# TensorE in place of VectorE for the turns of q and x in blocks 1 and 2, and block 3's q loaded in block 1's down stage

## The chip, the cores and the metric

The kernel runs on one core of one Trainium2 chip. The metric is the device time of one execution in microseconds (us), lower is better. All data is float32.

## The reference

Linear attention with a normalization, followed by a gated feed-forward block. The attention's output is laid out as one row of 512 values per token.

```python
# q, k, v: (8 batches, 8 heads, 576, 64)
kv  = einsum('bhsd,bhse->bhde', k, v)
o   = einsum('bhsd,bhde->bhse', q, kv)
o   = o / sqrt(mean(o * o, axis=-1) + 1e-6) * g_norm
x   = o.transpose(0, 2, 1, 3).reshape(4608, 512)
g   = x @ w_gate                      # (512, 1536)
out = (g / (1 + exp(-g)) * (x @ w_val)) @ w_out   # w_out (1536, 512)
```

## The kernel before

**Blocks and stages.** The 4608 tokens are worked off in nine blocks (0 to 8) of 512. Block n has an *up* stage (the gate and value products into `h`, 1536 wide) and a *down* stage (`h` times `w_out`, stored to `out`). While block n's down stage runs, the attention of block n + 1 (`nxt`, an object of class `Att`) is computed between its products, so that x of the next block is ready when its up stage begins.

**Products.** Block 0's up stage is a plain product (`plain_up`, L1018). From block 1 on, products are split after Strassen and Winograd into seven products of half size, called P1 to P7, each with sums of operands. Class `Up` does this once for block 1; class `Inner` does it twice, one inside the other, from block 2 on (`DEEP = 2`); class `Down` does it for the down stage. All these matmuls are issued at L551 (`Quad.multiply`) or L714 (`Inner.multiply`). The order of the products in the down stage is the list in `Ffn.down`; after a product p, `fill[p]` runs a piece of the next block's attention.

**The weights' stream.** The inner products need sums of weight pieces ("leaves"). They are made once, in block 1, by `leaf_steps` on VectorE (the steps show as L111 and L112) and written to DRAM by SP's queue (L823). From block 2 on `Stream.pump` loads them from there into `t` tiles (L795), as fast as these nine tiles come free; `Stream.enable`, called behind P7 of the down stage before, begins this. The leaves of the last two of six weight tiles (j = 4 and 5) are in `latest` and made in block 1's down stage, behind P5 in the x pool's `xi` tile and behind P7 in a tile of its own. Block 2's own sums of x, `xi`, are written into that same `xi` tile afterwards.

**Loads of q and k, v.** They pass through a pool `ld` of four tiles. All of these loads, the leaves and the stores go through SP's queue, in one order.

**The next block's attention.** `TURNED` and `quarters` choose between two ways of turning q and x (tokens on partitions) into q and x with features on partitions:

- With `quarters`, q is loaded in pieces of 32 by 32 (`load_quarters`, L282: two DMAs for most pieces, 32 for a block's q), turned within these squares by one VectorE step for each half (L329), and needs no TensorE. Without it, q is loaded in rows (L298), turned by 16 TensorE transposes (L335) and copied out of PSUM by VectorE (L339) or ScalarE (L337).
- From block `TURNED` on, `steps` runs `whole` behind P1: the product of q and kv in one piece (L355), its squares (L366) and sums (L367), one inverse root (`root`, 11 small VectorE steps, L373 to L385), the scaling (L113), and two VectorE turns (`blocks_x`, L412). Behind P5 `place_x` moves the 32-wide squares to their places by 16 DMAs on SP and ACT (L426), and behind P2 `gain_x` (L433) and `sums` follow. Before block `TURNED`, the block is done in two halves: `half(0)` behind P1, `middle` behind P6 (`turn_x(0)` and `half(1)`) and `last` behind P2 (`turn_x(1)` and `sums`). `turn_x` turns by 8 TensorE transposes (L402) and two ScalarE copies with the gain (L403).

In the kernel before, `TURNED` is 1 and `quarters` holds for every block but 0, so block 0 alone uses TensorE for turns.

**Order.** The program is written in the order above; a scheduler then sets the order of instructions of each engine by its own costs. `tc.issue_after(...)` lets the code in its body be ordered only behind a given instruction. `t2` prepares the weights that block 1's products use, in block 0's down stage; `turn_t(p)` makes three tiles of weight differences on GpSimd for the down stage's products P5, P7 and P4; P4's waits for the next block's first half. PSUM pools: `a` 1 tile, `b` 3, `c` 2, `m` 2.

Of the kernel before, what the change touches and what calls it, by code (L numbers as in the profile page):

```python
# [8 lines left out]
F32 = mybir.dt.float32  # L9
# [5 lines left out]
P = 128  # L15
# [3 lines left out]
def kernel(  # L19
# [41 lines left out]
    nc = tc.nc  # L61
# [22 lines left out]
    ld_pool = pool("ld", 4)  # L84
# [27 lines left out]
    sub = lambda e, o, a, b: e.tensor_tensor(out=o, in0=a, in1=b, op=OP.subtract)  # L112
    mul = lambda e, o, a, b: e.tensor_tensor(out=o, in0=a, in1=b, op=OP.mult)  # L113

    def ring():

        return r_pool.tile([P, 4, BLK], F32, name="r")
# [75 lines left out]
    class Att:  # L193


        def __init__(self, n):
            self.n = n

            self.cut, half = divmod(n, 2)
            self.split = half * D  # L200
            self.ps, self.z = {}, None
            self.q, self.k, self.v, self.room = [], {}, {}, None
            self.halves = []
            self.quarters = n > 0

        def parts(self, t):

# [58 lines left out]
                    )  # L266
                    views[j] = t.rearrange("p h (t d) -> p h t d", t=KT)

        def load_quarters(self, i, pairs=(0, 1)):


            if pairs[0] == 0:
                self.q.append(ld_pool.tile([P, LD], F32, name="ld")[:, 0 : 2 * BLK])
            to = self.q[i].rearrange("p (j g d) -> p j g d", j=2, d=P // 4)
            cut = 2 * self.n
            spans = [(self.n - 1, S - D * self.n, 0, cut), (self.n, 0, cut, BLK // 32)]
            for j in pairs:
                for r in range(4):
                    h, d = divmod(r, 2)
                    for b, s0, g0, g1 in spans:  # L280
                        if g1 > g0:
                            nc.sync.dma_start(  # L282
                                out=to[32 * r : 32 * (r + 1), j, g0:g1],
                                in_=q[b, 4 * i + 2 * j + h, s0 : s0 + 32 * (g1 - g0), 32 * d : 32 * (d + 1)].rearrange(
                                    "(g p) d -> p g d", p=32
                                ),
                            )

        def load_q(self, i):
            if self.quarters:  # L290
# [127 lines left out]
        def place_x(self):  # L418
            src = self.turned.rearrange("p i (x c) -> p (i x) c", c=P)
            self.x = x_pool.tile([P, 7, 2, HB], F32, name="x")  # L420
            dst = self.x[:, 0:4].rearrange("p o k (t c) -> p (o k t) c", c=P)
            rows = [slice(32 * r, 32 * (r + 1)) for r in range(4)]
            for a in range(4):
                for b in range(4):
                    queue = nc.scalar if b % 2 else nc.sync
                    placed = queue.dma_start(out=dst[rows[b], :, rows[a]], in_=src[rows[a], :, rows[b]])  # L426
                    if b % 2 == 0:
                        self.placed = placed

        def gain_x(self):  # L430
            for i in range(2):
# [93 lines left out]

    DEEP = 2

    TURNED = 1

    class Quad:  # L530

# [41 lines left out]
    class Up(Quad):  # L573
# [51 lines left out]
        def multiply(self, p):  # L625
            super().multiply(p)
            ffn = self.ffn
            if ffn.n != DEEP - 1:
                return

            if p == 5:
                self.leaf_room = ring().rearrange("p f (s c) -> p (f s) c", c=P)
            if p in (5, 7, 4):
                at = 3 * (5, 7, 4).index(p)
                ffn.making.extend(leaf_steps(self.j, [(self.w[p].unsqueeze(1), (p,))], self.leaf_room[:, at:]))
            if p == 3:
                if ffn.leaf_room is None:
                    ffn.leaf_room = x_pool.tile([P, 3, 7, P], F32, name="xi").rearrange("p a b c -> p (a b) c")
                halves = lambda t: t[self.j].rearrange("p (o i) c -> p o i c", o=2)
                steps = lambda room: leaf_steps(self.j, [(halves(wg), (1, 2)), (halves(wv), (6, 3))], room)  # L640
                if self.j < NP - 2:
                    ffn.later.extend(steps(ffn.leaf_room))
                else:
                    ffn.latest.append(steps)

# [195 lines left out]
    class Down(Quad):  # L841
# [51 lines left out]
        def after2(self):  # L893
            add(nc.vector, self.o1[:, :, 0:HD], self.ps["a"], self.s)
            if self.final:
                self.ffn.store(self.o1[:, :, 0:HD], 0, slice(0, HD))

            pairs = self.ffn.h.rearrange("p (j e) t -> p e j t", e=2)
            self.s4 = sub(nc.vector, pairs[:, 1, :, 0:HB], pairs[:, 1, :, 0:HB], pairs[:, 0, :, HB:BLK])

        def after7(self):
            o = ring()
# [25 lines left out]
    class Ffn:  # L928
# [52 lines left out]
        def down(self, nxt):  # L981

            down = self.down_
            fill = nxt.steps() if nxt else {}
            for p in (1, 6, 5, 7, 2, 4, 3) if 5 in fill else (1, 5, 6, 7, 2, 4, 3):
                if p == 1:
                    down.turn_t(7, self.ended)
                if p == 6:
                    down.turn_t(4, nxt.halves[0] if nxt and nxt.n >= TURNED else None)

                with tc.issue_after(nxt.multiplied.ins) if self.n == 0 and p in (5, 6) else ExitStack():
                    down.multiply(p)
                self.make(12)
                if p in fill:
                    fill[p]()
                if p in (5, 7) and self.n == DEEP - 1:

                    with tc.issue_after(nxt.scaled.ins), tc.issue_after(nxt.placed.ins):
                        room = self.leaf_room if p == 5 else ring().rearrange("p f (s c) -> p (f s) c", c=P)
                        for step in self.latest.pop(0)(room):  # L1000
                            step()
                if p == 1:

                    with tc.issue_after(nxt.q_turned.ins) if self.n == 0 else ExitStack():
                        down.turn_s3()
# [60 lines left out]
    for n in range(NB):  # L1066
        ffn = Ffn(n, blocks[n])
        nxt = blocks[n + 1] if n + 1 < NB else None
        if n == 0:

            with tc.issue_after(squared.ins), tc.issue_after(scaled.ins):
                weights(2)
            ffn.plain_up(0, (0,))
            copied = blocks[0].copied
            blocks[0].turn_x(1)
            for f in range(NF):
                with tc.issue_after(blocks[0].copied.ins if f else copied.ins):
# [12 lines left out]
            ffn.plain_end()  # L1090
            for g in range(2):
                nxt.kv(g)
        else:

            def third():
                nxt.kv(0)
                nxt.load_kv(1)

            def two_thirds():
                nxt.kv(1)  # L1100
                if nxt.n == 2:
# [12 lines left out]
        if DEEP <= n < NB - 2:  # L1114
            for i in range(2):
                blocks[n + 2].load_q(i)
        ffn.down(nxt)
        if n == 0:
            blocks[2].load_kv(0)

            with tc.issue_after(nxt.halves[0].ins):
                for j in range(NP // 2):
                    t2(wv[j][:, 0:2], wv[j][:, 2:4], wg[j][:, 0:2])
            with tc.issue_after(ffn.down_.s4.ins):
                for j in range(NP // 2, NP):
                    t2(wv[j][:, 0:2], wv[j][:, 2:4], wg[j][:, 0:2])


# [29 lines left out]
```

## Time and profile before

| what | value |
|---|---|
| time, median of 3 runs | 1025.14 us (1025.01 to 1025.32) |
| the profiled execution's own time | 1025.01 us |
| its span | 1023.2 us |
| TensorE (PE) busy | 1006.5 us, 98% |
| VectorE (DVE) busy | 701.0 us, 69% |
| ScalarE (ACT) / GpSimd (POOL) busy | 228.0 / 368.9 us |
| granted TensorE clock | 1.00 |

The page gives the busy time of each engine, the share of each in the chain of work that ended last, and groups of instructions by source line. The busy sum of PE is of the records' lengths laid over each other; matmuls are pipelined, so what one costs is read from the distance between starts. In an answer of the timeline a row is: start, length, engine, line, operation, out <- in, shape, count, and in brackets how long the engine was idle before it and who released it. In the waits a row is: total us, how often, the longest. SPq and ACTq are the queues in which an engine issues DMAs. A line L111, L112 or L113 is that of a helper (add, subtract, multiply) and tells the operation only.

### The profile page before, as it was taken

Reading aid. Unit: us, or ns where it says so; the run is one execution under the profiler, and the core shown is the slowest. Engines: PE = TensorE matmul, PEld = TensorE weight load, DVE = VectorE, ACT = ScalarE, POOL = GpSimd, SP = SyncE. Lnnn points to the kernel's source line nnn. Section 1 sums busy time; section 2 is a strip of 40 time slices with the busy share of each in tenths; the row PEclk is TensorE's granted clock in tenths of the full one; section 3 lists DMA queues with packets and bytes.
Section 4 is the critical chain, followed back from the end, with each engine's and each line's share of the span. In section 5 each row is a group of like instructions: output and inputs, shape, how many; then the busy total and the mean of one; then the engine's idle time right before and its main releaser. Section 6 shows DMA issues by size and latency. Waiting matters only on the chain.

```text
span 1023.2 us, 21404 instructions
## 1 busy us (share of the span) xinstructions
PE 1006.5 (98%) x8522; PEld 896.9 (88%) x8522; DVE 701.0 (69%) x1168; ACT 228.0 (22%) x352; POOL 368.9 (36%) x280
## 2 busy tenths in 40 slices
PE   6999999999999999999999999999999999999998
PEld 4544688888999989998999899988998999989997
DVE  2999688998666945685657566665669466946661
ACT  2766111221211212121121211111121211211110
POOL 0000263434045512561246315630555046513670
PEclk9999999999999999999999999999999999999999
DMA  8689633667888367855685568637772766066601
GB/s 224 201 264 275 127 70 113 184 150 167 246 219 245 70 164 204 253 100 119 209 243 146 89 199 246 183 57 200 231 197 50 175 196 188 20 165 205 189 29 42
DMA packets 273844, 170.26 MB, mean 166 GB/s; under 512 B 150608, under 2 KB 241872, under 8 KB 273744
## 3 DMA queue, kind: packets, MB, share of 16 engines
q1 hardware_dynamic: 238800, 164.42, 59.4%
q10 hardware_dynamic: 34880, 4.46, 2.7%
q8 instruction: 68, 1.11, 0.5%
q14 instruction: 32, 0.26, 0.1%
q0 software_dynamic: 64, 0.00, 0.0%
HBM read 138.02 MB, written 22.41 MB: 157 GB/s over the span
## 4 chain that ended last, share of the span: by engine, by line
PE 92%; DVE 3%; DMA 2%; SPq 1%; issue 1%; ACT 1%; DVEq 0%; ACTq 0%
PE b L714 26%; PE b L551 20%; PE c L714 13%; PE c L551 10%; PE a L714 6%; PE a L551 5%; PE b L1018 4%; PE c L1018 4%; PE m L314 2%; PE m L355 1%; DMA h<-in_v_dram 1%; SPq L282 1%; DVE xi L112 1%; DVE r L111 1%; DMA h<-in_k_dram 0%
## 5 line engine op out<-in xcount | busy, mean ns | idle before, releaser
L111 POOL TENSOR_TENSOR r<-r 128x256 f32<-128x256 f32 (+1 forms) x105 | 110.8, 1062 | 301.0 <-DVE r L111 241.1
L111 DVE TENSOR_TENSOR r<-b,r 128x512 f32<-128x512 f32 (+1 forms) x273 | 161.9, 606 | 65.6 <-PE b L714 60.6
L112 POOL TENSOR_TENSOR t<-wo 128x512 f32<-128x512 f32 x81 | 114.5, 1437 | 213.4 <-DVE wo L111 103.5
L111 DVE TENSOR_TENSOR r<-c,r 128x512 f32<-128x512 f32 (+1 forms) x179 | 108.4, 617 | 88.1 <-PE c L714 54.5
L714 PE MATMUL b<-x,t 128*128 128x128 f32 x1092 | 151.2, 275 | 0.0
L111 DVE TENSOR_TENSOR r<-a,r 128x512 f32<-128x512 f32 (+1 forms) x99 | 62.5, 631 | 113.5 <-PE a L551 71.1
L714 PEld LDWEIGHTS b<-x,t 128*128 128x128 f32 x1092 | 136.5, 192 | 0.8
L714 PE MATMUL c<-xi,t 128*128 128x128 f32 x840 | 112.4, 275 | 0.4 <-DVE xi L111 0.4
L113 POOL TENSOR_TENSOR h<-r 128x1024 f32<-128x1024 f32 (+1 forms) x40 | 81.9, 2064 | 78.1 <-DVE r L111 75.4
L714 PEld LDWEIGHTS c<-xi,t 128*128 128x128 f32 x840 | 102.9, 192 | 0.5 <-DVE xi L111 0.5
L551 PE MATMUL b<-wo,h 128*128 128x256 f32 x432 | 100.0, 383 | 0.1
L551 PE MATMUL b<-t,h 128*128 128x256 f32 x432 | 96.9, 381 | 0.0
L551 PEld LDWEIGHTS b<-t,h 128*128 128x128 f32 x432 | 81.5, 190 | 11.4 <-issue 0.2
L551 PEld LDWEIGHTS b<-wo,h 128*128 128x128 f32 x432 | 79.8, 190 | 13.0 <-DVE h L113 2.5
L728 ACT COPY r<-b 128x512 f32<-128x512 f32 x63 | 36.9, 586 | 211.5 <-PE b L714 206.4
L714 PE MATMUL b<-xi,t 128*128 128x128 f32 x588 | 79.7, 276 | 0.0
L714 PEld LDWEIGHTS b<-xi,t 128*128 128x128 f32 x588 | 72.4, 192 | 0.0
L714 PE MATMUL b<-x,wg 128*128 128x128 f32 x336 | 52.7, 279 | 0.2 <-DVE x L112 0.2
L714 PE MATMUL b<-x,wv 128*128 128x128 f32 x336 | 51.3, 275 | 0.0
L551 PE MATMUL a<-wo,h 128*128 128x256 f32 x216 | 48.3, 379 | 0.0
L551 PE MATMUL c<-wo,h 128*128 128x256 f32 x216 | 48.1, 379 | 0.0
L551 PE MATMUL c<-t,s 128*128 128x256 f32 x216 | 48.1, 379 | 0.0
(128 smaller groups left out, 1556.8 us busy)
## 6 DMA issues: line engine op xcount, KB each, us to landing
t<-w SPq DMA_DIRECT2D x336, 256.0 KB, 3.6
out_dram<-r SPq DMA_DIRECT2D x17, 512.0 KB, 3.1
ld<-in_k_dram SPq DMA_DIRECT2D x26, 288.0 KB, 5.3
ld<-in_v_dram SPq DMA_DIRECT2D x26, 288.0 KB, 6.3
ld<-in_moe_w_gate_dram SPq DMA_DIRECT2D x12, 512.0 KB, 4.9
ld<-in_moe_w_val_dram SPq DMA_DIRECT2D x12, 512.0 KB, 4.8
ld<-in_moe_w_out_dram SPq DMA_DIRECT2D x12, 512.0 KB, 5.0
w<-t SPq DMA_DIRECT2D x18, 256.0 KB, 3.3
```

What stands on the lines that cost most here:

```text
L111: add = lambda e, o, a, b: e.tensor_tensor(out=o, in0=a, in1=b, op=OP.add)
L112: sub = lambda e, o, a, b: e.tensor_tensor(out=o, in0=a, in1=b, op=OP.subtract)
L113: mul = lambda e, o, a, b: e.tensor_tensor(out=o, in0=a, in1=b, op=OP.mult)
L282: nc.sync.dma_start(out=to[32 * r : 32 * (r + 1), j, g0:g1], in_=q[b, 4 * i + 2 * j + h, s0 : s0 + 32 * (g1 - g0), 32 * d : 32 * (d + 1)]. ...
L314: nc.tensor.matmul(self.kv_ps[r][u * D : (u + 1) * D, g, :], lhsT=k[:, u, c, :], rhs=v[:, u, c, :], start=(c == 0), stop=(c == KT - 1),)
L355: self.multiplied = nc.tensor.matmul(self.ps[i][u][p : p + D, t, j, :], lhsT=self.qt[rows, 2 * i + t, j, p : p + D], rhs=kvs[b % 3][rows, ...
L551: nc.tensor.matmul(banks[e][:, e], lhsT=lhsT, rhs=rhs, start=first and i == 0 and (e == 0 or banks[0] is not banks[1]), stop=i == self.ste ...
L714: nc.tensor.matmul(ps[:, i, f], lhsT=self.weight(o, p, f), rhs=self.operand(o, p), start=first and (i, f) == (0, 0), stop=True, skip_group ...
L728: nc.scalar.copy(out=dst, in_=ps)
L1018: nc.tensor.matmul(t, lhsT=w[f // 2][:, i, P * (f % 2) : P * (f % 2 + 1)], rhs=x[:, i, of], start=(i == 0), stop=(i == NS - 1),)
```

## The change

In short, what the change does:

1. `TURNED` becomes 3, and `quarters` holds for block 1 and for blocks 3 to 8. Block 1's x, block 2's q and block 2's x are turned by TensorE; block 1's q and all of blocks 3 to 8 as before. The down stages of blocks 0 and 1 take the order P1, P5, P6, P7, P2, P4, P3 in place of P1, P6, P5, P7, P2, P4, P3, with the attention of the next block in two halves.
2. Block 3's q is loaded behind P5 of block 1's down stage in place of four parts in block 2's up stage.
3. The leaves of j = 4 and 5 are made behind P1 and P7, both in the `xi` tile, and wait for the scaling alone.
4. `t2` for the last three of six weight tiles waits for the first half of block 1's attention instead of the sums behind P2 (`s4`); `turn_t(4)` in blocks 0 and 1 waits for no half.

The name of the change speaks of the stream's loads behind P7; the line that begins them (`if p == 7: stream.enable(...)`) is in both kernels.

```diff
-            self.quarters = n > 0
+            self.quarters = n == 1 or n >= TURNED
...
-        def load_quarters(self, i, pairs=(0, 1)):
...
+        def load_quarters(self, i):
...
-                    placed = queue.dma_start(out=dst[rows[b], :, rows[a]], in_=src[rows[a], :, rows[b]])
-                    if b % 2 == 0:
-                        self.placed = placed
+                    queue.dma_start(out=dst[rows[b], :, rows[a]], in_=src[rows[a], :, rows[b]])
...
-    TURNED = 1
+    TURNED = 3
...
-                steps = lambda room: leaf_steps(self.j, [(halves(wg), (1, 2)), (halves(wv), (6, 3))], room)
+                steps = leaf_steps(self.j, [(halves(wg), (1, 2)), (halves(wv), (6, 3))], ffn.leaf_room)
                 if self.j < NP - 2:
-                    ffn.later.extend(steps(ffn.leaf_room))
+                    ffn.later.extend(steps)
                 else:
                     ffn.latest.append(steps)
...
                 self.make(12)
+                if p == 5 and self.n == DEEP - 1:
+                    for i in range(2):
+                        self.loads(i)
                 if p in fill:
                     fill[p]()
-                if p in (5, 7) and self.n == DEEP - 1:
-
-                    with tc.issue_after(nxt.scaled.ins), tc.issue_after(nxt.placed.ins):
-                        room = self.leaf_room if p == 5 else ring().rearrange("p f (s c) -> p (f s) c", c=P)
-                        for step in self.latest.pop(0)(room):
+                if p in (1, 7) and self.latest:
+
+                    with tc.issue_after(nxt.scaled.ins):
+                        for step in self.latest.pop(0):
                             step()
...
-                if nxt.n == 2:
+                if nxt.n < TURNED:
                     for i in range(2):
                         nxt.load_q(i)
-            fill = {4: third, 8: two_thirds} if nxt else {}
-            if n == DEEP:
-                for a, at in enumerate((1, 2, 3, 5)):
-                    fill[at] = lambda i=a // 2, j=a % 2: nxt.load_quarters(i, (j,))
-            ffn.up(fill)
+            ffn.up({4: third, 8: two_thirds} if nxt else {})
...
-        if DEEP <= n < NB - 2:
-            for i in range(2):
-                blocks[n + 2].load_q(i)
+        if TURNED - 2 <= n < NB - 2:
+            ffn.loads = blocks[n + 2].load_q
+            if n >= DEEP:
+                for i in range(2):
+                    ffn.loads(i)
...
             with tc.issue_after(nxt.halves[0].ins):
-                for j in range(NP // 2):
-                    t2(wv[j][:, 0:2], wv[j][:, 2:4], wg[j][:, 0:2])
-            with tc.issue_after(ffn.down_.s4.ins):
-                for j in range(NP // 2, NP):
+                for j in range(NP):
                     t2(wv[j][:, 0:2], wv[j][:, 2:4], wg[j][:, 0:2])
```

More of the change, by code (lines that the diff above doesn't have):

```diff
@@ L267, in load_kv @@
                     views[j] = t.rearrange("p h (t d) -> p h t d", t=KT)
-        def load_quarters(self, i, pairs=(0, 1)):
-            if pairs[0] == 0:
-                self.q.append(ld_pool.tile([P, LD], F32, name="ld")[:, 0 : 2 * BLK])
-            to = self.q[i].rearrange("p (j g d) -> p j g d", j=2, d=P // 4)
+        def load_quarters(self, i):
+            ld = ld_pool.tile([P, LD], F32, name="ld")[:, 0 : 2 * BLK]
+            to = ld.rearrange("p (j g d) -> p j g d", j=2, d=P // 4)
             cut = 2 * self.n
             spans = [(self.n - 1, S - D * self.n, 0, cut), (self.n, 0, cut, BLK // 32)]
-            for j in pairs:
+            for j in range(2):
                 for r in range(4):
@@ L287, in load_quarters @@
                             )
+            self.q.append(ld)
         def load_q(self, i):
@@ L898, in after2 @@
             pairs = self.ffn.h.rearrange("p (j e) t -> p e j t", e=2)
-            self.s4 = sub(nc.vector, pairs[:, 1, :, 0:HB], pairs[:, 1, :, 0:HB], pairs[:, 0, :, HB:BLK])
+            sub(nc.vector, pairs[:, 1, :, 0:HB], pairs[:, 1, :, 0:HB], pairs[:, 0, :, HB:BLK])
         def after7(self):
```

## The prediction, made before the changed kernel ran

> **What bounds the kernel now.** I read the page first, for the busy shares:
>
> ```profile
> PE 1006.5 (98%) x8522; PEld 896.9 (88%) x8522; DVE 701.0 (69%) x1168; ACT 228.0 (22%) x352; POOL 368.9 (36%) x280
> PEclk9999999999999999999999999999999999999999
> PE 92%; DVE 3%; DMA 2%; SPq 1%; issue 1%; ACT 1%; DVEq 0%; ACTq 0%
> ```
>
> TensorE is busy for 98% of the span, at a clock that never drops, and is 92% of the chain that ended last. Whatever is put on TensorE lengthens the run unless it falls into a gap, so next I asked the waits of PE for its gaps:
>
> ```profile
> PE m L248 <- DMA h<-in_v_dram: 4.7, 2, 3.9
> PE b L335 <- DMA ld<-in_q_dram: 4.3, 1, 4.3
> PE c L551 <- DVE r L111: 1.6, 3, 0.7
> PE c L714 <- DVE xi L111: 0.4, 1, 0.4
> ```
>
> The two large waits are the first loads at the kernel's start, which the change leaves alone. In the part that it touches, from 114 us (end of block 0's gate and value products) to 273 us (start of block 2's), only the third row stands; the fourth lies at 597 us. The windows of those stages say the same:
>
> ```profile
> 114.00:156.00 42.00, 42.00 (x476) 36.83 (x476) 35.84 (x45) 7.04 (x12) 17.53 (x12) 1.00 0.49 101
> 156.00:229.00 73.00, 71.92 (x432) 62.26 (x431) 66.23 (x124) 15.80 (x29) 29.10 (x22) 1.00 0.57 150
> 229.00:273.00 44.00, 43.45 (x350) 37.28 (x349) 35.87 (x65) 8.41 (x13) 12.79 (x9) 1.00 0.85 207
> ```
>
> Columns: length, PE, PEld, DVE, ACT, POOL busy, clock, DMA share, GB/s. PE loses 1.6 us in 159. In its timeline each wait also spoils the pipeline around it: groups of 8 normally start 1.73 us apart, but 2.23, 2.63 and 2.52 us lie before the three that waited, and 1.83 behind. That is 0.6 + 1.0 + 0.9, some 2.5 us: all that this stage could give back.
>
> **The change, part by part.**
>
> *Transposes put on TensorE.* Block 1's x, block 2's q and block 2's x are turned by TensorE again: 16 transposes of 128x128 each, 48 in all. Block 0 does the same already, at L402; its timeline is the price list:
>
> ```profile
> 28.34 1.06 PE L402 MATMUL m<-ident,r 128*128 128x128 f32 x8 [0.28 <-DVE r L113]
> 31.57 0.93 PE L402 MATMUL m<-ident,r 128*128 128x128 f32 x7
> 32.59 1.99 PE L1018 MATMUL c<-x,wv 128*128 128x256 f32 x8
> 34.42 0.27 PE L402 MATMUL m<-ident,r 128*128 128x128 f32 x1
> 36.72 1.89 PE L1018 MATMUL c<-x,wv 128*128 128x256 f32 x8
> 38.44 1.88 PE L1018 MATMUL b<-x,wg 128*128 128x512 f32 x4
> ```
>
> One takes 0.27 us alone; 8 take 1.06, so they follow at (1.06 - 0.27) / 7 = 0.113 us. Seven end their issue at 31.57 + 7 x 0.113 = 32.36, and the next matmul starts at 32.59: 0.23 us of change-over. The group behind takes 1.83 (32.59 to 34.42) instead of 1.72 (36.72 to 38.44): 0.11 more. A group of n costs 0.113 n + 0.34. The built order has six groups: 8 + 8 for block 1, 6 + 10 for block 2's q around the last P4 and P3 of block 1's up stage, 8 + 8 for block 2's x. Sum: 48 x 0.113 + 6 x 0.34 = **7.5 us**. They stand between matmuls that run without a gap, so nothing hides them. From below, 48 x 0.113 without change-overs is 5.4; from above, none pipelined, 48 x 0.27 is 13.0. I stay at 7.5: the row is the same instruction in the same kernel.
>
> The Trainium skill speaks for the change in "VectorE: DVE Perf Modes", section "The three transpose paths" (390 ns for a full 128x128 turn on TensorE against 311 ns on VectorE for 32x32 blocks only), but its page "TensorE: Matmul & The Clock Gate", section "Part 4: PE-mode transpose", gives 275 ns in a kernel and says that the clock gate does not count transposes as busy. By that figure the sum would be an estimated 13.2 us. The rows above agree with it as the length of one (0.27 us), not as its spacing (0.113 us), and the granted clock stood at 1.00 beside them.
>
> *The product of q and kv split in two* (blocks 1 and 2): half follows P1, half the first 8 transposes behind P6. The 64 pairs now take 2.03 us in one piece (121.79 to 123.82); a second entry costs about 0.2 (the first matmul after a change takes 0.20 in the chain, the others 0.04 at most). 2 x 0.2 = **0.4 us**. The second half also needs an m bank that ScalarE must first empty: copy of P6 0.59, L403 0.68, so about 1.3 us against 1.24 + 0.15 of work before it; 0.1 each, **0.2 us**.
>
> *Taken off VectorE:* L412 in blocks 1 and 2 (2.4 us each) and block 2's L329 (2 x 1.2); added: a second root chain in each (11 small steps, 126.35 to 128.88: 2.5 us) and one copy (0.69). Balance: 7.2 - 5.7 = 1.5 us less, of an engine that only matters where PE waits for it. That is where L329 stands ahead of an add:
>
> ```profile
> 228.67 1.22 DVE L329 STREAM_TRANSPOSE r<-ld 128x1024 f32<-128x1024 f32 x1
> 229.82 0.65 DVE L111 TENSOR_TENSOR r<-a,r 128x512 f32<-128x512 f32 x1
> 232.31 1.99 PE c L551 x8
> ```
>
> The third wait should go: **-0.9 us**. The other two come from leaf steps at L112, which stay; between keeping all (0) and losing all (-2.5) I take -0.9, the one with a named cause.
>
> *Taken off the queues:* `place_x` of both blocks, 16 DMAs each on SP and ACT (7.2 us of issue from 250.75), and `gain_x`. PE never waited there: 0. ScalarE gains 8 L403 (0.68) and 3 copies for 4 L433 (1.1), under its 22%: 0.
>
> *Block 3's q.* Its 32 DMAs leave block 2's up stage (16 before it, 16 among its weight loads) and stand together in SP's queue in block 1's down stage, ahead of the stream's first loads and of the last leaf writes; block 2's q becomes 4 DMAs in place of 32. An issue took 0.6 to 0.77 us (16 in 9.55; 15 in 11.50), so the 32 hold SP for 19 to 25 us. P7's trigger of the stream is the same in both kernels. From the row times moved by the terms above: they start near 240, wait at 256 for the leaves of j = 4, and end near 267; six weight loads (0.87 each) follow until 272, landing 3.6 later, the first near 271. Block 2 starts near 272.9 + 6.5 = 279. So they are covered by 8 us: 0; each microsecond beyond those 8 would be one of waiting.
>
> *The last leaves.* j = 5 is now made in the same xi tile as j = 4 and behind it, and block 2's own xi is that tile again. Its two writes are queued behind those six loads: issued near 273, landed 3.9 later, at 277; the first xi sum ends at 278. P5 of block 2 reads it near 280. Slack 2 us; bounds 0 to +4 (SP at 0.77 instead of 0.6 to 0.7, and landings of 5 us as other loads show).
>
> *Block 1's second half of x.* VectorE makes twelve `t2` steps between the two roots: 0.62 each alone, 1.2 beside GpSimd (six in 7.2 us from 133.57). The scale then ends between 142 and 149; turn_x(1) is due at 147. Middle 144, in time; bounds 0 to +2. GpSimd's `turn_t(4)` no longer waits for the first half (17.7 us of wait at 131.44): its 3 x 1.25 us move to 114, beside `h_sums` and the q turn of block 1, which has 1 us to spare before its product. GpSimd beside it took a 1536-wide step from 1.76 to 2.25, so +0.5 per step: bounds 0 to +1. I take **+0.3** for both.
>
> The rule "SBUF: two separate sides" on the Trainium skill's page "SBUF — State Buffer" is harder: a VectorE step with two SBUF inputs blocks for a whole GpSimd step. By it the three steps would cost up to an estimated 3.7 us; the rows show 0.5 to 0.6 us lost per step.
>
> Sum: 7.5 + 0.4 + 0.2 - 0.9 + 0.3 = **+7.5 us**. The profiled run took 1025.01 us for a span of 1023.2, 1.8 around it; the median of the runs is 1025.14. Forecast 1025.0 + 7.5 = **1032.5 us**.
>
> **The rivals.** (a) *Block 2 starts late* through SP: if the 32 q loads go at 0.77 or more, with leaf writes behind them, xi or the first weights come 2 to 5 us after PE is ready: 1034.5 to 1037.5. For it: everything shares one queue, and DMA is already 0.85 busy there. Against it: 2 us of slack for xi and 8 for the weights.
> (b) *The relief is larger:* change-overs vanish in the pipeline and all three waits of VectorE go: 5.4 + 0.6 - 2.5 = +3.5, 1028.5. Against it: two of the waits have leaf steps as their cause.
> (c) *Not slower:* the transposes slip in beside the matmuls as the 64x64 products do (records 0.22 us long, 0.015 apart), costing 48 x 0.015 = 0.7, while the three waits go: -1.8, 1023.2. It decides from a spacing under (2.5 + 2) / 48 = 0.09 us. Block 0's row shows 0.113 with full-size transposes, so it needs another behaviour of the same instruction.
> (d) *The change does not do what its name says:* the stream's trigger behind P7 is not touched, so no gain or loss comes of that; what is left is the rest of the sum. This is my forecast's own reading, not a separate time.
>
> **How the numbers follow.** Forecast (1031 to 1034.4) 0.66; (a) 0.22; (b) 0.09; (c) 0.03. What is measurable is about 0.2%, 2 us: (b) is beyond it, (c) is split between faster and same. Chances: faster 0.01, same 0.04, slower 0.95. The range reaches from (b)'s upper half, 1029.0, to the end of (a), 1037.5.
>
> **What would show it.** Right: L402 with 48 rows and L335 with 32 in all, at 0.11 spacing; no L412 before block 2's down stage; block 1 starting 2.9 us later (156.0 to about 158.9), block 2 near 279.5; the stage from there to the end as long as before. The forecast is wrong if the second stage loses or gains more than 2 us by waits of PE for DVE, if PE waits for xi or t at block 2's start, or if blocks 3 to 8 take another time.

## The result and the profile after

The changed kernel takes 1030.27 us (median of 4 runs, 1030.12 to 1031.38) against 1025.23 (1025.01 to 1026.59) for the kernel before, measured side by side: ratio 1.0049, 95% interval 1.0031 to 1.0066. It is 5.0 us slower. The forecast was 1032.5 (1029.0 to 1037.5): the sign and the range held, the time was forecast 2.2 us too long (+7.5 against +5.0).

Everything that follows is read by stages. A stage is the distance between the first product matmuls of two stages in PE's timeline; the time ahead of it, with the first loads, is not in it: it differs by up to 2.2 us between the traces (115.46 to 117.64). ("Block 0, down" runs from P1 of block 0's down stage to the first product of block 1, "block 1" from there to the first of block 2, and so on.)

| stage, us | before | changed | difference |
|---|---|---|---|
| block 0, down | 39.51 | 41.52 | +2.01 |
| block 1 | 116.89 | 119.80 | +2.91 |
| block 2 | 108.49 | 108.31 | -0.18 |
| blocks 3 to 8 | 638.67 | 638.67 | 0.00 |

So blocks 3 to 8 are untouched, to a hundredth, and the whole loss lies where the transposes were put. The page of the changed kernel, at the lines shown of before:

```profile
PE 1012.8 (98%) x8570; PEld 904.0 (88%) x8570; DVE 703.3 (68%) x1185; ACT 230.0 (22%) x359; POOL 371.1 (36%) x280
PE 93%; DVE 4%; DMA 2%; issue 1%; ACT 1%; SPq 0%; DVEq 0%; ACTq 0%
```

TensorE has 48 records and 6.3 us of busy time more. VectorE has not become freer, 703.3 us in place of 701.0: what left it (L412, two L329) was replaced by a second root chain, and steps beside GpSimd became longer. SPq's share of the chain went from 1% to 0%; block 2's q now costs it 4 issues in place of 32. The waits of PE for VectorE in the changed part went from 1.6 us in three to 0.7 in one, while the wait of 0.4 us for `xi`, which lies in a later block, stayed:

```profile
PE c L549 <- DVE r L111: 0.7, 1, 0.7
```

(L549 and L712 are L551 and L714 of the kernel before, L793, L821 and L281 its L795, L823 and L282.) The timeline of PE around the two turns of block 1's x:

```profile
134.04 1.04 PE L402 MATMUL m<-ident,r 128*128 128x128 f32 x8
135.01 0.56 PE L355 MATMUL b<-kv,r 64*64 64x64 f32 x10
136.55 5.45 PE L549 MATMUL b<-t,h 128*128 128x256 f32 x24
147.01 1.04 PE L402 MATMUL m<-ident,r 128*128 128x128 f32 x8
147.89 2.32 PE L549 MATMUL b<-t,h 128*128 128x256 f32 x10
```

From start to start, eight transposes take 0.97 and 0.88 us, not the 8 x 0.113 + 0.34 = 1.24 of the forecast. The second half of the product of q and kv, though, takes 1.54 us (135.01 to 136.55), where the whole product took 2.03 in one piece before.

The signs that the forecast named for itself are there: L402 has 48 rows and L335 has 32, L412 first runs in block 2's down stage (363 us), PE waits for neither xi nor t at block 2's start, and blocks 3 to 8 take the same time.

### The profile page after: what moved, and what is told of

It is laid out like the page before. It is cut to its first block, busy times and chain, and to the rows that moved or that the text cites. A ratio compares the mean times of both kernels' runs of the same rounds, so it can differ in the third digit from the quotient of the medians.

```text
span 1028.4 us, 21439 instructions
## 1 busy us (share of the span) xinstructions
PE 1012.8 (98%) x8570; PEld 904.0 (88%) x8570; DVE 703.3 (68%) x1185; ACT 230.0 (22%) x359; POOL 371.1 (36%) x280
## 3 DMA queue, kind: packets, MB, share of 16 engines
q10 hardware_dynamic: 26432, 3.41, 2.0%
q8 instruction: 68, 1.11, 0.4%
## 4 chain that ended last, share of the span: by engine, by line
PE 93%; DVE 4%; DMA 2%; issue 1%; ACT 1%; SPq 0%; DVEq 0%; ACTq 0%
PE b L712 26%; PE b L549 20%; PE c L712 13%; PE c L549 10%; PE a L712 6%; PE a L549 5%; PE b L1018 4%; PE c L1018 4%; PE m L314 1%; PE m L355 1%; DMA h<-in_v_dram 1%; DVE r L112 1%; DVE xi L112 1%; DVE r L111 1%; PE c L480 1%
## 5 line engine op out<-in xcount | busy, mean ns | idle before, releaser
L112 POOL TENSOR_TENSOR t<-wo 128x512 f32<-128x512 f32 x81 | 117.0, 1468 | 188.9 <-DVE wo L111 104.6
L712 PE MATMUL b<-x,t 128*128 128x128 f32 x1092 | 151.0, 275 | 0.0
L712 PEld LDWEIGHTS b<-x,t 128*128 128x128 f32 x1092 | 136.5, 192 | 0.6 <-DVE r L111 0.2
L712 PE MATMUL c<-xi,t 128*128 128x128 f32 x840 | 112.2, 275 | 0.4 <-DVE xi L111 0.4
L712 PEld LDWEIGHTS c<-xi,t 128*128 128x128 f32 x840 | 102.8, 192 | 0.5 <-DVE xi L111 0.5
L549 PE MATMUL b<-wo,h 128*128 128x256 f32 x432 | 99.5, 382 | 0.1
L549 PE MATMUL b<-t,h 128*128 128x256 f32 x432 | 96.9, 381 | 0.0
L549 PEld LDWEIGHTS b<-t,h 128*128 128x128 f32 x432 | 81.4, 190 | 11.3 <-issue 0.2
L549 PEld LDWEIGHTS b<-wo,h 128*128 128x128 f32 x432 | 80.0, 190 | 12.7 <-DVE h L113 2.5
L712 PE MATMUL b<-xi,t 128*128 128x128 f32 x588 | 79.7, 276 | 0.0
L712 PEld LDWEIGHTS b<-xi,t 128*128 128x128 f32 x588 | 72.4, 192 | 0.0
L712 PE MATMUL b<-x,wg 128*128 128x128 f32 x336 | 52.7, 279 | 0.2 <-DVE x L112 0.2
L712 PE MATMUL b<-x,wv 128*128 128x128 f32 x336 | 51.4, 275 | 0.0
L549 PE MATMUL c<-t,s 128*128 128x256 f32 x216 | 48.3, 380 | 0.0
L549 PE MATMUL a<-wo,h 128*128 128x256 f32 x216 | 48.3, 379 | 0.0
L549 PE MATMUL c<-wo,h 128*128 128x256 f32 x216 | 48.1, 379 | 0.0
```

The source lines that it names most:

```text
L549: nc.tensor.matmul(banks[e][:, e], lhsT=lhsT, rhs=rhs, start=first and i == 0 and (e == 0 or banks[0] is not banks[1]), stop=i == self.ste ...
L712: nc.tensor.matmul(ps[:, i, f], lhsT=self.weight(o, p, f), rhs=self.operand(o, p), start=first and (i, f) == (0, 0), stop=True, skip_group ...
```

## The experiments

Each kernel ran beside the kernel before, whose median was 1025.05 us for the first four of the table, 1024.87 for x1_alone, moved_loads, kv_whole and kv_whole_q_late, and 1024.89 for the last four. There is one trace of each kernel. This table has the medians, their ratio to before with its interval, and the stages of the profiled run:

| kernel | us | ratio (95%) | block 0, down | block 1 | block 2 | 3 to 8 |
|---|---|---|---|---|---|---|
| twice | 1035.71 | 1.0105 (1.0091 to 1.0118) | 42.78 | 122.97 | 108.30 | 638.80 |
| second_half_b | 1030.35 | 1.0052 (1.0039 to 1.0064) | 41.40 | 119.50 | 108.30 | 638.67 |
| x1_only | 1033.03 | 1.0081 (1.0067 to 1.0095) | 42.28 | 116.79 | 112.68 | 638.79 |
| q2_vector | 1031.95 | 1.0065 (1.0052 to 1.0077) | 41.85 | 117.48 | 112.09 | 638.82 |
| x1_alone | 1027.22 | 1.0027 (1.0018 to 1.0036) | 42.12 | 115.93 | 108.49 | 638.84 |
| moved_loads | 1033.60 | 1.0080 (1.0067 to 1.0094) | 43.75 | 117.05 | 111.95 | 638.67 |
| kv_whole | 1022.44 | 0.9978 (0.9969 to 0.9987) | 39.41 | 115.85 | 107.59 | 638.87 |
| kv_whole_q_late | 1022.22 | 0.9973 (0.9962 to 0.9983) | 38.58 | 115.06 | 107.60 | 638.66 |
| q3_back | 1030.79 | 1.0054 (1.0041 to 1.0066) | 41.92 | 119.80 | 108.31 | 638.66 |
| turn_t4_waits | 1036.95 | 1.0115 (1.0101 to 1.0128) | 47.40 | 119.79 | 108.31 | 638.67 |
| changed_kv_whole | 1029.59 | 1.0043 (1.0030 to 1.0056) | 41.37 | 119.80 | 107.38 | 638.97 |
| best | 1022.94 | 0.9976 (0.9966 to 0.9986) | 38.89 | 115.08 | 107.60 | 639.09 |

**twice: what a transpose costs.** In the changed kernel:

```diff
-                    nc.tensor.transpose(ps[:, j], self.q[t][:, j], ident)
+                    [nc.tensor.transpose(ps[:, j], self.q[t][:, j], ident) for _ in range(2 if self.n else 1)]
...
-                        nc.tensor.transpose(ps[:, e, t], xt[:, t, j + e], ident)
+                        [nc.tensor.transpose(ps[:, e, t], xt[:, t, j + e], ident) for _ in range(2 if self.n else 1)]
```

> The changed kernel with each of its 48 added transposes issued twice, in the same groups; the second copy writes the same values. This measures a transpose without the edges of its group. Spacing theory (a transpose costs the 0.113 us at which it follows the one before, and the edge of a group next to nothing): 48 x 0.113 = +5.4 us on the changed kernel, 1035.7. The forecast's own reading says the same of the second copies, +5.4, since no group is added; what it says of the edges (6 x 0.34 = 2.0) must then show in the first copies. Length theory (0.27 us each, nothing overlapped): +13, 1043.3. Overlap theory (0.015 apart, as the 64x64 products): +0.7, 1031.0.

Measured: 1035.71, 5.4 us above the changed kernel's 1030.27. Its timeline at the same two places:

```profile
134.44 1.91 PE L402 MATMUL m<-ident,r 128*128 128x128 f32 x16
136.28 0.39 PE L355 MATMUL m<-kv,r 64*64 64x64 f32 x6
147.82 1.91 PE L402 MATMUL m<-ident,r 128*128 128x128 f32 x16
149.57 0.60 PE L549 MATMUL b<-t,h 128*128 128x256 f32 x2
```

Sixteen take 1.84 and 1.75, so the added eight cost 0.87 in both: 0.109 each. What is left of 0.97 and 0.88 for the edge of a group is 0.1 and 0.0. The length theory (0.27 each) and the overlap theory (0.015) are both out. The stages grew by 1.26 and 3.17, less than 16 and 32 x 0.109, because the product behind the longer turn (136.28 to 137.36) fell from 1.54 to 1.08: it begins with the m bank, which ScalarE has had time to empty. That is a first sign of why the split product is dear. So the close hit of the time (1035.71 for 1035.7) is partly luck: by the stages the kernel grew by some 4.5 us only.

**second_half_b: the split product.**

```diff
-                self.half(1, (m_psum, b_psum))
+                self.half(1, (b_psum, b_psum))
```

> The changed kernel with both banks of the second half's product of q and kv taken from pool b, so that it need not wait until ScalarE has emptied an m bank. Bank theory (the second half takes 1.54 us in place of about 1.03 because its first ten matmuls must go to one bank, 0.046 us apart, while ScalarE empties the other): -0.5 us in each of the two blocks, -1.0 in all, 1029.3. Rival, the split itself (two entries into a chain of small matmuls cost what they cost, whatever the bank): 0, 1030.3. Rival, b is needed by the products around it: later, up to +1, 1031.3.

```profile
135.40 0.93 PE L355 MATMUL b<-kv,r 64*64 64x64 f32 x48
136.25 5.45 PE L549 MATMUL b<-t,h 128*128 128x256 f32 x24
147.36 1.06 PE L402 MATMUL m<-ident,r 128*128 128x128 f32 x8 [0.47 <-DVE r L113]
```

The second half now takes 0.85 us (135.40 to 136.25) in place of 1.54, but it has 48 matmuls here, where the changed kernel has 56: 16 and 8 of its 64 stand within the first half. In block 2, where both kernels have all 64 in one place, it takes 1.10 (255.32 to 256.42) in place of 1.54, so the bank theory holds for the product, with nearly the 0.5 expected. In the code each half of a product's rows goes to a bank of its own, so ten matmuls in one bank are also ten on the same 64 rows: the runs don't tell which of the two sets them 0.046 us apart. The kernel hardly gains (block 0's and block 1's stages -0.12 and -0.30, the time none), for in block 0's down stage PE now reaches `turn_x(1)` before VectorE has scaled x and waits 0.47 us, as the bracket of the third row says. In the changed kernel that scaling ends 0.3 us before it is due: whatever is saved ahead of it comes back as a wait.

**x1_only and q2_vector: single turns.** Both are the changed kernel with less on TensorE:

```diff
 x1_only:
-    TURNED = 3
+    TURNED = 2
...
-                if nxt.n < TURNED:
+                if nxt.n == 2:
 q2_vector:
-            self.quarters = n == 1 or n >= TURNED
+            self.quarters = n > 0
```

> The changed kernel with only block 1's x turned by TensorE; block 2's q and x go back to VectorE, and block 2's q is loaded in pieces again. Block 3's q and the last leaves stay where the change put them. Against the kernel before, by what the changed kernel's trace shows: 16 transposes 1.9, the split of the product 1.1, two kv products in fewer pieces -0.7, VectorE's third wait still there 0: +2.3, 1027.5. By the forecast's terms: 16 x 0.113 + 2 x 0.34 + 0.2 + 0.1 + 0.3 = +3.1, 1028.3. If the moved loads and leaves cost something by themselves, more than either.

> The changed kernel with block 2's q turned by VectorE again; x of blocks 1 and 2 stays on TensorE. What the changed kernel has on top is block 2's q: 16 transposes, and VectorE's third wait gone. By its trace: 2.0 of transposes less 1.2 of waits, so this kernel is 0.8 us faster than the changed one, 1029.5. By the forecast's terms: 16 x 0.113 + 2 x 0.34 - 0.9 = 1.6 us, 1028.7. If the waits that went were worth all 2.5: this kernel is slower, 1030.8.

Both missed, and not in the transposes. With fewer of them these kernels are slower than the changed one, by some 2.8 and 1.7 us, and the stage that gives it away is block 2: 112.68 and 112.09 in place of 108.31. There PE waits for `xi`. In order, the last leaf writes, the first sum of xi and the first product with it, in x1_only (with `place_x` ahead of them) and then in the changed kernel:

```profile
265.05 6.12 SPq L426 DMA_DIRECT2D x<-r  x8
274.43 1.01 SPq L821 DMA_DIRECT2D w<-xi  x2
281.42 1.09 DVE L111 TENSOR_TENSOR xi<-x 128x896 f32<-128x896 f32 x1 [0.87 <-DMA w<-xi]
282.56 3.62 PE L712 MATMUL c<-xi,t 128*128 128x128 f32 x16 [2.74 <-DVE xi L111]
```

```profile
265.59 1.00 SPq L821 DMA_DIRECT2D w<-xi  x2
273.34 1.09 DVE L111 TENSOR_TENSOR xi<-x 128x896 f32<-128x896 f32 x1 [1.32 <-DMA w<-xi]
278.94 1.06 PE L712 MATMUL c<-xi,t 128*128 128x128 f32 x8
```

In both the sum is released by the leaf write's DMA. In the changed kernel it ends at 274.43, 4.5 us before PE reads xi; in x1_only the write is issued 8.8 us later and there is no slack left. This is the forecast's rival (a), in full, in kernels that keep the moved loads and leaves but turn less of block 2 on TensorE. Between the two pairs of leaf writes, SP's queue holds 12 of block 3's loads (7.85 us, from 257.10), 8 issues of `place_x` for block 2 (the first row) and 6 weight loads in x1_only. The changed kernel has the same there without `place_x`, which goes when TensorE turns x (its 12 loads take 6.72 us, from 255.77): that row is 6.1 of the 8.8 us. q2_vector has no `place_x` either, but 20 of block 3's loads (12.00 us, from 255.97) where the changed kernel has 12. SP stood idle from 246.7 to 254.6 there, so it is the order built, not a full queue, that puts 8 more loads behind the first pair. Both kernels also load block 2's q in 32 issues instead of 4, but these lie at 183 to 221 us; that they are the cause of the later order isn't shown.

**x1_alone: the transposes without the moves.** The kernel before, with one line changed:

```diff
-    TURNED = 1
+    TURNED = 2
```

> The kernel before with TURNED = 2 and nothing else: block 1's x turned by TensorE, block 3's q still loaded within block 2's up stage. Queue theory (x1_only lost 4.2 us in block 2 because block 3's q, 32 DMAs, stands ahead of the last leaf writes in SP's queue): nothing is lost in block 2 here; block 0's down stage is 2.0 to 2.8 us longer as in the runs so far, one kv product in one piece gives back 0.35: 1027.0 to 1027.6. If instead the later scaling of x makes the leaves late: as x1_only, about 1032. By the forecast's terms: +3.1, 1028.2.

Measured 1027.22, as the queue theory said (1027.0 to 1027.6). Block 2 takes 108.49, the very time of before: the later scaling of x does no harm by itself, and x1_only's 4.2 us need the moved loads and leaves. Which of the two was not run alone: with the leaves of j = 5 in a tile of their own, as here, the first sum of xi (270.78) is not released by the last leaf write at all. The price is +2.61 in block 0's down stage, and -0.96 comes back in block 1, where the waits for VectorE fall from 1.6 to 0.7 us and two kv pieces become one. Of the +2.61, some 0.6 has nothing to do with a transpose:

```profile
121.58 1.25 DVE L329 STREAM_TRANSPOSE r<-ld 128x1024 f32<-128x1024 f32 x1 [0.67 <-DMA ld<-in_q_dram]
122.88 0.27 PE L355 MATMUL m<-kv,r 64*64 64x64 f32 x1 [0.52 <-DVE r L329]
```

The last of block 1's 32 q loads lands late, VectorE's turn waits for it, and PE waits for the turn in the middle of the first half. From the matmul before to this one it is 0.74 us, in the changed kernel 0.13, and in x1_only, for the same reason, 0.89. In q3_back it is 0.53; there not the load is late but VectorE, whose two 1536-wide steps take 2.68 and 2.71 us beside GpSimd. Without these differences the four stages agree at 41.5 us. How much of this wait belongs to a kernel and how much to a single execution, one trace of each doesn't tell.

**moved_loads: the moves without the transposes.** The changed kernel with

```diff
-    TURNED = 3
+    TURNED = 1
...
-                if nxt.n < TURNED:
+                if nxt.n == 2:
```

> The change without its first part: TURNED stays 1 and VectorE turns q and x of all blocks from 1 on; block 3's q is loaded behind P5 of block 1's down stage, both last leaves are made in the xi tile, t2 and turn_t(4) wait as in the changed kernel or before where TURNED decides. Queue theory: SP reaches the last two leaf writes 4 to 8 us later, block 2's first product with xi waits 2 to 5 us for them: 1027 to 1030. The forecast's terms for these parts (0 for the loads, 0 for the leaves): 1025.1.

Measured 1033.60: 8.7 us above before and 3.3 above the changed kernel. The forecast had 0 for these parts. Block 2 loses 3.46 us as expected, again with 12 loads and `place_x` ahead in SP's queue, with the last leaf write issued at 277.67 and PE waiting 3.00 us for xi at 286.50. Block 0's down stage loses another 4.24, which was not expected: PE waits 2.29 us for an add of VectorE, and the matmuls behind it are slow.

```profile
154.42 7.13 PE L549 MATMUL c<-wo,h 128*128 128x256 f32 x24 [2.29 <-DVE r L111]
154.50:158.00 3.50, 3.50 (x10) 2.86 (x11) 2.92 (x4) 0.00 (x0) 0.39 (x1) 0.60 0.40 150
```

The second row is a window, with the columns of the forecast's windows: the granted clock is 0.60 there. P3 takes 6.97 us to the next start where it takes 5.18 elsewhere, so the wait of 2.29 cost 4.1. The add was late because all twelve `t2` steps now stood in VectorE ahead of it, from 134.86 to 151.01, beside GpSimd's `turn_t(4)` and the steps behind that.

**turn_t4_waits: that collision by itself.** The changed kernel with the old wait:

```diff
-                    down.turn_t(4, nxt.halves[0] if nxt and nxt.n >= TURNED else None)
+                    down.turn_t(4, nxt.halves[0] if nxt else None)
```

> The changed kernel with turn_t(4) of blocks 0 and 1 waiting for the first half of the next block's attention, as it waited before. GpSimd's three steps then no longer stand beside VectorE's h_sums and q turn. Port theory (two steps of 1536 took 2.28 and 2.71 in place of 1.76 each, so that the first half's product came late and took 0.37 more than in block 2): -0.4 us, 1029.9; the forecast had +0.3 for this and the twelve t2 steps. Rival: the three steps then delay P4 or the weights t of block 1: up to +1.

Both readings were wrong, and by far: 1036.95, 6.7 us more, 5.9 of it in block 0's down stage. The first half did not get shorter either (1.74 us in place of 1.47): VectorE's first 1536-wide step takes 2.90 here, beside the last of GpSimd's six steps for the products P5 and P7, and block 1's q lands late.

```profile
130.59 4.99 POOL L112 TENSOR_TENSOR t<-wo 128x512 f32<-128x512 f32 x3 [13.05 <-DVE r L113]
139.41 3.43 DVE L111 TENSOR_TENSOR wv<-wv,wg 128x512 f32<-128x512 f32 x2
142.26 3.38 POOL L112 TENSOR_TENSOR t<-wg,wv 128x512 f32<-128x512 f32 x2
152.42 1.94 PE L402 MATMUL m<-ident,r 128*128 128x128 f32 x8 [4.08 <-DVE r L113]
```

GpSimd's three steps have moved from 114 to 130.59, into the `t2` steps. A `t2` step takes 1.72 us there (3.43 for two) and a GpSimd step beside it 1.69, where VectorE alone needs 0.62. The twelve end near 147.4 in place of 140.8, x is scaled 4 us late, PE waits 4.08 for it, and the granted clock is 0.50 from 152 to 154. So dropping this wait, which `TURNED` = 3 does in a line that both kernels have, keeps the rest of the change at +5.

**q3_back: block 3's q in the changed kernel.**

```diff
-                if p == 5 and self.n == DEEP - 1:
-                    for i in range(2):
-                        self.loads(i)
...
+            if n == DEEP:
+                for a, at in enumerate((1, 2, 3, 5)):
+                    fill[at] = lambda i=a // 2, j=a % 2: nxt.load_quarters(i, (j,))
```

> The changed kernel with block 3's q loaded in block 2's up stage again, in four parts, as in the kernel before; all else as changed. In the changed kernel the sums of xi end 4.5 us before the product that needs them, so queue theory and the forecast both say that these loads cost nothing there: 1030.3. If they do cost (SP or DMA shares in block 1's down stage): faster, down to 1029. If taking block 2's q loads out of SP's queue was what paid for them, the slack of xi must grow here by about the time of 32 issues, 17 us, or to where something else sets it.

1030.79 against 1030.27, with blocks 1 and 2 the same to a hundredth; the 0.4 us in block 0's down stage are a longer wait for the turn of block 1's q. But the loads did not move back: in the order that was built, SP issues all 32 of block 3's q between 238.43 and 270.6, before block 2 begins at 279.36 and among the weight loads now. So this run doesn't test whether the loads belong in block 2. That they cost nothing in the changed kernel rests on that kernel itself: its block 2 is 0.18 us shorter than before, and PE waits for nothing at its start. The slack of xi grew from 4.5 to 5.8 us (the first sum ends at 274.46, PE reads xi at 280.25), not by 17; it is the adds of x ahead of the sum in VectorE, no longer a leaf write, that release it.

**kv_whole, kv_whole_q_late, changed_kv_whole, best: what the waits and the pieces are worth without a transpose.** `third` and `two_thirds` issue the product of k and v of the next block. The scheduler hoists part of it to where TensorE is free by its own costs, and so cuts it into pieces. The edits (the second in kv_whole_q_late and best alone; changed_kv_whole and best leave out block 6 by `if n != 5`):

```diff
+                with tc.issue_after(ffn.sent.ins):       # the last product matmul issued
-                nxt.kv(0)
+                    nxt.kv(0)
...
-            nxt.turn()
+            with tc.issue_after(ffn.added.ins) if n == 1 else ExitStack():   # the last add behind P7
+                nxt.turn()
```

> The kernel before with the product of k and v of the next block ordered only behind the last matmul in front of it, so that the scheduler does not issue half of it earlier: 20 pieces become 12. Piece theory (two pieces of 34 and 38 take 0.72 + 0.74, one of 72 takes 1.21, and the group behind a piece 0.1 more): 8 x -0.35 = -2.8 us, 1022.3. Rival, the pieces fill time that PE would lose anyway: 0, 1025.1.

> kv_whole, and VectorE's turn of block 2's q ordered behind the last add of block 1's up stage. That takes away the third of the three waits of PE for VectorE as the change did, without a transpose on TensorE: -0.9 us on kv_whole, 1021.4. If the wait only moves to the add behind, or the product of q and kv now waits for the turn: kv_whole's time or up to 1 us more.

> The changed kernel with kv in whole pieces, as kv_whole, but block 6's left as it is (there the later kv cost 1.2 us in kv_whole: loads of q stood ahead of place_x in SP's queue, and PE waited 1.0 for xi). Blocks 2 and 3 are whole in the changed kernel already, so only blocks 4, 5 and 7 are left to gain: by the stages of kv_whole -0.4, -0.4 and 0, 1029.5; by the count of pieces (17 to 13) -1.4, 1028.9.

> The kernel before with kv in whole pieces in all blocks but 6 and the q turn of block 2 held until the last add of block 1's up stage; nothing of the change. kv_whole_q_late lost 1.3 us in block 6 and won 0.4 in block 5, which this takes back: 1022.2 - 0.9 = 1021.3. If block 6's loss had another cause: 1022.2.

In the kernel before, a piece of 34 in block 0's down stage (the next matmul starts at 145.38); in kv_whole, the whole in block 1's up stage (the next at 179.01):

```profile
144.66 0.79 PE L314 MATMUL m<-ld 64*64 64x64 f32 x34
```

```profile
177.81 1.28 PE L314 MATMUL m<-ld 64*64 64x64 f32 x72
```

34 take 0.72 and 72 take 1.20, so two pieces (34 + 38, 1.46) cost 0.26 more than one, and each spoils the group behind it by 0.1. kv_whole is 2.4 us faster than before (expected 2.8): blocks 1 and 2 give 1.9, but block 6 loses 1.2 (109.63 in place of 108.43). Block 0's down stage would give some 0.7 more, if in its trace PE had not waited 0.82 us from one matmul to the next for block 1's q, as in x1_alone. Holding the q turn takes another 0.79 out of block 1, close to the forecast's 0.9 for that wait; in the times, 1022.22 against 1022.44, it does not show. changed_kv_whole gives 1029.59, as the stages of kv_whole said; its runs (1028.15 to 1030.97) overlap those of the changed kernel. best gave 1022.94 and not 1021.3: sparing block 6's own kv did not help. In all three kernels without block 7's early piece PE waits 1.04 us for xi in block 6 where before it waited 0.39; the piece of 34 that stood ahead of block 6, at the end of block 5's down stage, is gone, so PE arrives earlier, and the rest of xi's chain, it seems, does not. It would have to be block 7's kv that stays cut; that was not run. kv_whole, kv_whole_q_late and best all beat both kernels and can't be told apart by their times.

## Why the prediction was right, and where its sum was wrong

| term | forecast | measured | from |
|---|---|---|---|
| transposes and edges | +7.5 | +5.8 | six groups in the changed kernel, start to start |
| split product and its m bank | +0.6 | +1.8 | 1.47 + 1.54 and 1.10 + 1.54 against 2.03 twice, and 0.1 behind each added entry |
| waits for VectorE in block 1 | -0.9 | -1.2 | spoiled spacing 2.5 before, 1.3 after |
| block 1's half of x, `turn_t(4)` | +0.3 | in the row above | under 0.1 of the first half's 1.47 |
| kv pieces | not named | -1.05 | seven pieces become four in blocks 2 and 3 |
| block 3's loads, leaves, `place_x` | 0 | 0 | block 2's stage, -0.18; 4.5 us of slack for xi |

The measured terms come to +5.3; the stages say +4.7 and the times +5.0. Of the difference nothing more can be named. That TensorE would pay for its transposes, and that nothing would hide them, was right. That the sum came within 2.5 us was in part luck: a term three times too small stood against one too large and one that was missing.

**Transposes: right kind, wrong edge.** The spacing of 0.113 was right (0.109 in twice), and so was its being unhidden. The step that failed is the change-over of 0.34 a group, read from block 0, where the next matmul followed 0.23 us late. PE's own rows show no wait there, but the weight load's row, of the kernel before, does:

```profile
32.59 1.59 PEld L1018 LDWEIGHTS c<-x,wv 128*128 128x128 f32 x8 [0.33 <-DVE wv L162]
```

VectorE was still writing the matmul's weights (L162, until 32.53). A wait of that one place was priced as a property of the instruction, six times. In the changed kernel the edges add up to some 0.6 us (5.8 less 48 x 0.109), where 2.0 was forecast. The 390 and 311 ns that the forecast quotes from the Trainium skill's page "VectorE: DVE Perf Modes" stand there for bf16; the data here is float32.

**The split product** was priced by its second entry alone, 0.2 each, and 0.1 each for the m bank. Two things make it dearer. Ten matmuls in a row go to one b bank 0.046 us apart, where alternating banks (and rows) follow at 0.015, because the other bank is the m bank that ScalarE is still emptying until 135.4 (twice and second_half_b: 1.54 to 1.08 and 1.10 without that). And in block 1 the first half takes 0.37 more than in block 2, because eight matmuls of the second half stand within it, all in one bank; the second half, with 56 left, still takes 1.54. The expectation of turn_t4_waits put these 0.37 on VectorE's steps beside GpSimd. The trace leaves under 0.1 for that: behind the eight, the next matmul starts 0.05 us after q's turn ends, and 0.13 after the matmul before it.

**kv pieces** were not in the sum at all. The built order of the changed kernel shows them, as rows of L314; the forecast looked only at the instructions that the diff names.

**Rival (a)** had 0.22 and did not happen, but x1_only, q2_vector and moved_loads show its mechanism at 3.5 to 4.2 us. The forecast's reason against it (slack) held: 4.5 us for xi where it had estimated 2. It gave the removal of `place_x` from the queues 0, because PE had never waited there; in x1_only its 8 issues for block 2 are 6.1 of the 8.8 us by which the last leaf write comes late. So the term is 0 only beside moves that would need that time. **Rival (b)**, with change-overs gone and all three waits gone (+3.5), was half right: the change-overs did vanish, one wait of three stayed. **Rival (c)** is refuted by twice. **(d)** holds: the line that triggers the stream is unchanged, SP issues the first six of its loads from 262.60 (before: one at 248.26 and five from 260.82), and no gain shows in block 2.

**The parts do not add up.** Alone, the moves cost 8.7 us (moved_loads); with the transposes added to them, the whole costs 5.0. Turning block 2's q on TensorE costs PE 2.0 us in block 1; turning block 2's x there takes 8 issues of `place_x` out of the one queue in which the leaves wait, and turning block 1's x takes L412 out of VectorE, where `t2` and the adds wait. The forecast put the whole loss on the transposes and took the moves as free. Its time came out near because in this combination they are.

## What to carry to other kernels

Before a gap between two rows is taken as the price of an instruction, look at the weight loads' row beside it: a wait can stand there alone. When a change consists of parts, run the parts: here the moves alone cost more than the whole, and the slack of a few microseconds that made them free came from another part of the same diff. Look in the built order whether an edit did what it says: q3_back's did not. And compare the full built order of an engine, not only the lines of the diff: the pieces of a product that no line of this change names were worth 1 us, and keeping them whole made the original kernel 2.4 us faster.

## What the runs showed of the hardware

A wait of PE can cost more than its length. Behind waits of 1.99 us (q2_vector), 2.29 (moved_loads), 2.74 (x1_only) and 4.08 (turn_t4_waits) the granted clock stood at 0.50 for 3.41 us each time, while behind waits of 0.39 to 1.04 it stayed at 1.00, and behind one of 3.00 (moved_loads, 286.50) too. Windows of q2_vector (two rows), and those around the wait of 3.00 in moved_loads, with the columns of the forecast's windows:

```profile
277.58:280.99 3.41, 1.42 (x13) 1.23 (x12) 2.32 (x3) 0.59 (x1) 0.00 (x0) 1.00 0.79 296
281.00:284.41 3.41, 3.41 (x18) 3.41 (x18) 3.05 (x4) 0.59 (x1) 0.00 (x0) 0.50 0.60 191
281.52:284.92 3.40, 1.98 (x16) 1.64 (x14) 2.08 (x3) 0.00 (x0) 0.47 (x1) 1.00 1.12 371
284.94:288.34 3.40, 1.84 (x16) 1.84 (x17) 2.96 (x3) 0.59 (x1) 0.23 (x1) 1.00 0.98 368
```

The first two are cut where the clock changes, the last two by counting on in steps of 3.41 us from 155.23, where the clock changed in moved_loads. The stretches just ahead of a low clock have PE busy for 1.42 us or less of 3.41 (q2_vector 1.42, moved_loads 1.11, x1_only 0.77, turn_t4_waits 0.00). With the steps counted from the first entry of each trace's clock record, no other stretch has PE busy for less than 2.3 us but the last two rows above. (Waits before 12 us, of 3.4 to 5.1, say nothing here: the record of the clock begins between 15 and 23 us.) The wait of 3.00 falls across a boundary and leaves 1.98 and 1.84 us busy in the stretches on its two sides. So what these traces suggest is a clock that is set anew every 3.41 us by how busy PE was in the stretch before, with the limit somewhere between 1.42 and 1.84 us; it is five waits in four traces, and no run was made to test it. The Trainium skill's page "TensorE: Matmul & The Clock Gate", section "Part 1: The HAM clock gate (the "warmup" mystery)", has the clock halve after an idle window of about 3.4 us that runs freely. The halving and the length of the window agree; but a window did not have to be idle throughout: 1.99 us without a matmul in it were enough.

VectorE and GpSimd slowed each other more than the forecast took from the trace: 1.72 us for a 512-wide `t2` step beside GpSimd's 1.69 in turn_t4_waits, against 0.62 alone, a loss of 1.1 and not the 0.5 to 0.6 that it set against the rule in the section "SBUF: two separate sides" of the Trainium skill's page "SBUF — State Buffer". The kernel before has such steps too (1.75 us at 137.30); the forecast's 1.2 is a mean over these and steps that ran alone. In turn_t4_waits the two rows of nearly equal length look like the taking of turns that the rule describes; the 1536-wide steps of the changed kernel (2.28 and 2.71 against 1.76) lost 0.5 and 0.95.
